# Moving one tile's tail rows forward and issuing 63 matrix products in halves, in a kernel that streams products

## The chip, the cores and the metric

One core of one Trainium2 chip. The metric is the device time of that core in microseconds (us), the lower the better. Times are medians of several executions; a trace of one execution belongs to each kernel. The experiments ran in four batches on four chips (1 to 4, 5 to 8, 9 to 11, and 12), each beside the kernel before on the same chip, so gains are differences within a batch. Before the change the kernel took 476.81 us (median of three runs, 476.67 to 477.1).

## The reference

A cross network of six layers on a batch of 16384 rows by 416 columns, all in bf16:

```python
def reference(x0, ws, bs):            # (16384, 416), (6, 416, 416), (6, 416)
    x = x0
    for l in range(6):
        proj = jnp.einsum('bd,de->be', x, ws[l]) + bs[l]
        x = x0 * proj + x
    return x
```

## The kernel before

The rows are cut into eight groups of 2048, held transposed (columns on the partitions). A group g in a layer l is a job (g, l). 416 columns are three input tiles of 128 and a tail of 32, so an output tile of 128 columns by 2048 rows needs, in four PSUM banks of 512 rows each, twelve full products (three input tiles t, four chunks j) and four products with the 32 tail rows, which use only 32 rows of the array and run side by side (in the trace of before 384 of 447 successive pairs of them start 2 to 5 ns apart, and the rest 215 to 217, the interval of full products):

```python
    def full(g, l, i, banks, first, chunk_major, after_chunk=None, chunks=range(NJ), ts_=range(NT)):
        ...
        for t, j in seq:
            add("pe", lambda h, t=t, j=j: h.matmul(
                bank(banks[j]), wm[l][:, t, ecols], src(t, j, j + 1),
                start=(first and t == 0), stop=(not first and t == NT - 1)),
                reads=[stok(t, j), ("wm", l)], writes=[("ps", banks[j])])
            ...

    def rows32(g, l, i, banks, first, small=False, inner=False):   # the tail rows
        ...                        # small: sixteen 32x32 pieces in place of four products
            add("pe", lambda h, q=q, j=j, r=r: h.matmul(
                bank(banks[j]), w3[l][q, ecols], src[q, :], start=first and not inner,
                stop=not first and not inner,
                tile_position=(r * T32, 0)),
                ...
```

ACT reads a finished tile out of PSUM and adds the bias (L398), DVE multiplies by x0 (L407) and adds x (L412). The kernel's eight banks hold two tiles, so a tile's banks must be read before the tile after the next can begin (two weight loads of before, at 24.54 and 25.55 us, came after 0.51 and 0.89 us of waiting for ACT's reads). Most tiles alternate: full products and then tail rows, next tail rows and then full products, so that two sets of tail rows meet. The first job is followed by the first two tiles of the second group, which have their own function, because their input is still arriving:

```python
    def two_tiles(g, l):
        ...
        bks = [job_banks(), job_banks()]
        for t in (0, 1):
            for i in (0, 1):
                full(g, l, i, bks[i], True, False, ts_=[t])
        full(g, l, 0, bks[0], True, False, ts_=[2])
        rows32(g, l, 0, bks[0], False)
        evacuate(g, l, 0, bks[0], list(range(NJ)), 2)
        finish_tile(g, l)
        rows32(g, l, 1, bks[1], False, inner=True)
        full(g, l, 1, bks[1], False, False, ts_=[2])
        evacuate(g, l, 1, bks[1], list(range(NJ)), 2)
        finish_tile(g, l)
```

At the end two things overlap. The output of the last group but one is turned to rows by transposing DMAs (`ost` from x, `ot` for the tail; ACT copies `ot` into `ost`) and then stored. The last job computes its rows directly and stores them in pieces:

```python
        turn(0); turn(1)                      # ost <- x, transposing DMA     (shortened)
        add("sp", lambda h: h.dma_start_transpose(ot3[:, :, :], x3s[s3][:, :]), ...)
        turn(2, 0, 2); turn(2, 2, NJ)
    ...
        if (g, l) == (LAST, L - 2) and i < NT - 1:
            if i:
                spread("act")                 # ost <- ot, on ACT
            rest_turn(i)                      # x <- x, transposing DMA for the last job
    ...
    store(LAST - 1, 0, 2)                     # out <- ost, the first stores of the end
    store(LAST - 1, 2, NJ)
```

## Time and profile before

| | before |
|---|---|
| time | 476.81 us; with later runs beside the experiments 477.1 |
| span of the profiled execution | 475.1 us |
| PE | 3344 matmuls and 3344 weight loads, busy 99% |
| DVE, ACT | busy 85% and 72% |
| instruction fetches (queue 8) | 26 packets, 0.43 MB |
| DMA | busy 49% of the span on average, but full from 460 to about 473 us |

PE has work in every slice of the profile, so whatever lengthens or shortens PE's stream should move the end. The prediction below shows the lines for that.

### The profile page before, as it was taken

How to read it: one execution, taken by the hardware profiler on the slowest of the kernel's cores; microseconds unless marked ns; L12 is line 12 of the kernel's file. 1: busy time of each engine (PE TensorE's matmuls, PEld its weight loads, DVE VectorE, ACT ScalarE, POOL GpSimd, SP SyncE). 2: the span in 40 equal slices, each digit the busy share in tenths (PEclk: the TensorE clock that was granted, in tenths of full speed). 3: DMA queues.
4: the chain of work that ended last, by engine and by line, in shares of the span. 5: the costliest groups of instructions: out<-in, count | busy, mean ns of one | idle time of the engine just before them, and what ended most of it. 6: DMA issues, size and time to landing. Idle time of an engine off the chain costs nothing.

```text
span 475.1 us, 8338 instructions
## 1 busy us (share of the span) xinstructions
PE 468.5 (99%) x3344; PEld 193.5 (41%) x3344; DVE 404.5 (85%) x699; ACT 342.1 (72%) x372; POOL 6.0 (1%) x15
## 2 busy tenths in 40 slices
PE   9999999999999999999999999999999999999995
PEld 5334444444444444444444444444444444444342
DVE  2888888888888888898889879888888888888896
ACT  4587777777777777777777777777777777777785
POOL 1000000000000000000000000000000000001000
PEclk9999999999999999999999999999999999999999
DMA  8996910720102397379318931980000039025998
GB/s 234 195 165 148 193 49 1 156 67 0 35 1 45 73 219 156 76 157 228 82 31 199 218 87 31 180 256 0 2 12 23 9 63 239 12 46 121 228 181 258
DMA packets 138651, 53.18 MB, mean 112 GB/s; under 512 B 112362, under 2 KB 138100, under 8 KB 138612
## 3 DMA queue, kind: packets, MB, share of 16 engines
q1 hardware_dynamic: 138456, 52.54, 48.9%
q8 instruction: 26, 0.43, 0.4%
q10 hardware_dynamic: 156, 0.11, 0.1%
q14 instruction: 13, 0.11, 0.1%
HBM read 5.97 MB, written 13.63 MB: 41 GB/s over the span
## 4 chain that ended last, share of the span: by engine, by line
PE 98%; ACT 1%; DVE 0%; issue 0%; DVEq 0%; POOL 0%; POOLq 0%
PE ps L460 78%; PE ps L481 7%; PE ps L502 7%; PE ps L858 2%; PE ps L475 1%; PE ps L561 1%; PE ps L581 1%; PE ps L493 1%; ACT tw L398 0%; PE ps L869 0%; PE ps L902 0%; ACT x L913 0%; DVE x L919 0%; DVE x L925 0%; PE ps L907 0%; PE ps L601 0%
## 5 line engine op out<-in xcount | busy, mean ns | idle before, releaser
L398 ACT ACTIVATE tw<-ps,bias 128x1024 bf16<-128x1024 f32 (+1 forms) x295 | 299.8, 1071 | 120.1 <-PE ps L481 81.9
L460 PE MATMUL ps<-x,wm 128*128 128x512 bf16 x1692 | 379.9, 380 | 0.4 <-ACT tw L398 0.4
L460 PEld LDWEIGHTS ps<-x,wm 128*128 128x128 bf16 x1692 | 158.6, 98 | 215.1 <-issue 28.2
L407 DVE TENSOR_TENSOR tw<-tw,x 128x1024 bf16<-128x1024 bf16 (+1 forms) x285 | 192.5, 683 | 53.1 <-ACT tw L398 52.7
L412 DVE TENSOR_TENSOR x<-tw,x 128x1024 bf16<-128x1024 bf16 (+1 forms) x285 | 183.1, 683 | 0.0
L481 PE MATMUL ps<-x,w 32*128 32x512 bf16 x512 | 39.2, 379 | 0.0
L502 PE MATMUL ps<-x,wm 128*32 128x512 bf16 x564 | 33.0, 380 | 0.0
L438 ACT ACTIVATE ts<-ps,bias 128x512 bf16<-128x512 f32 x47 | 28.8, 702 | 0.0
L442 DVE TENSOR_TENSOR x<-ts,x 128x512 bf16<-128x512 bf16 x47 | 18.8, 422 | 2.7 <-DMA x<-x 2.7
L502 PEld LDWEIGHTS ps<-x,wm 128*32 128x32 bf16 x564 | 13.8, 96 | 17.6 <-issue 5.3
L481 PEld LDWEIGHTS ps<-x,w 32*128 32x128 bf16 x512 | 7.8, 92 | 27.6 <-issue 27.1
L440 DVE TENSOR_TENSOR ts<-ts,x 128x512 bf16<-128x512 bf16 x47 | 18.7, 421 | 0.0
L701 POOL COPY ost<-ot 128x512 bf16<-128x512 bf16 x6 | 4.6, 764 | 422.8 <-DMA ot<-x 422.8
L858 PE MATMUL ps<-wm,x 128*128 128x416 bf16 x48 | 9.5, 340 | 0.0
L591 DVE COPY x<-ps 128x512 bf16<-128x512 bf16 x5 | 2.0, 423 | 8.3 <-PE ps L581 8.3
L913 ACT ACTIVATE x<-ps 128x416 bf16<-128x416 f32 x16 | 7.8, 527 | 1.7 <-PE ps L858 1.6
L593 ACT ACTIVATE x<-ps 128x512 bf16<-128x512 bf16 x7 | 3.8, 595 | 5.0 <-PE ps L581 5.0
L858 PEld LDWEIGHTS ps<-wm,x 128*128 128x128 bf16 x48 | 4.3, 98 | 4.2 <-issue 1.0
L493 PE MATMUL ps<-x,w 32*32 32x512 bf16 x188 | 5.9, 374 | 0.0
L475 PE MATMUL ps<-x,w 32*32 32x512 bf16 x208 | 5.6, 385 | 0.0
L919 DVE TENSOR_TENSOR x<-x,x 128x832 bf16<-128x832 bf16 (+1 forms) x10 | 4.9, 502 | 0.6 <-ACT x L913 0.4
L925 DVE TENSOR_TENSOR x<-x,x 128x832 bf16<-128x832 bf16 (+1 forms) x9 | 4.7, 541 | 0.2
(41 smaller groups left out, 33.9 us busy)
## 6 DMA issues: line engine op xcount, KB each, us to landing
out_dram<-ost SPq DMA_DIRECT2D x6, 1664.0 KB, 7.2
x<-x SPq DMA_DIRECT2D x24, 96.0 KB, 2.1
wm<-in_ws_dram SPq DMA_DIRECT2D x6, 312.0 KB, 3.2
x<-in_x_dram SPq DMA_DIRECT2D x8, 208.0 KB, 4.0
x<-in_x_dram SPq DMA_DIRECT2D x4, 416.0 KB, 7.9
out_dram<-ost SPq DMA_DIRECT2D x2, 832.0 KB, 7.1
x<-x SPq DMA_DIRECT2D x22, 64.0 KB, 2.1
out_dram<-x SPq DMA_DIRECT2D x3, 416.0 KB, 5.2
```

What stands on the lines that cost most here:

```text
L398: add("act", lambda h, a=a, w=w, b0=b0: h.activation(tw[r][:, a * CH:(a + w) * CH], psum[:, b0 * CH:(b0 + w) * CH], ACT_F.Identity, bias=b ...
L407: add("dve", lambda h, a=a, e=e: h.tensor_tensor(tw[r][:, a * CH:e * CH], tw[r][:, a * CH:e * CH], x0s[s0][:, i * GC + a * CH:i * GC + e * ...
L412: add("dve", lambda h, a=a, e=e: h.tensor_tensor(xs[so][:, i * GC + a * CH:i * GC + e * CH], tw[r][:, a * CH:e * CH], src(i, a, e), ALU.ad ...
L438: add("act", lambda h: h.activation(ts[r][:, :], bank(b), ACT_F.Identity, bias=bias[:, 3, l:l + 1], scale=1.0), reads=[("ps", b), "bias"], ...
L440: add("dve", lambda h: h.tensor_tensor(ts[r][:, :], ts[r][:, :], x03, ALU.mult), reads=[("ts", r)] + tok0, writes=[("ts", r)], release=True)
L442: add("dve", lambda h: h.tensor_tensor(x3s[so][:, :], ts[r][:, :], res, ALU.add), reads=[("ts", r)] + rtok, writes=[("x3", so), ("x3", so, ...
L460: add("pe", lambda h, t=t, j=j: h.matmul(bank(banks[j]), wm[l][:, t, ecols], src(t, j, j + 1), start=(first and t == 0), stop=(not first a ...
L475: add("pe", lambda h, q=q, j=j, r=r, c=c, o=o: h.matmul(psum[o, banks[j] * CH:(banks[j] + 1) * CH], w3[l][q, i * P + c * T32:i * P + (c + ...
L481: add("pe", lambda h, q=q, j=j, r=r: h.matmul(bank(banks[j]), w3[l][q, ecols], src[q, :], start=first and not inner, stop=not first and no ...
L493: add("pe", lambda h, l=l, b=b, s3=s3, ri=ri, qi=qi, ro=ro, qo=qo: h.matmul(psum[qo, b * CH:(b + 1) * CH], w3[l][qi, NT * P:D], s3[qi, :], ...
L502: add("pe", lambda h, t=t, j=j, src=src, l=l, b=b, ro=ro, qo=qo: h.matmul(psum[qo, b * CH:(b + 1) * CH], wm[l][:, t, NT * P:D], src(t, j, ...
L858: add("pe", lambda h, t=t: h.matmul(bank(b, n=D), xcol(t, j, kk), wm[l][:, t, :], start=(first and t == 0), stop=(not first and t == NT - 1)),
```

## The change

The first part moves the second tile's four products with its middle input tile behind the first tile's tail rows, so that the first tile is complete four products sooner. The second issues 63 full products of three later jobs as two of 256 columns each, with the same weights.

```diff
+    HALVES = ((1, 2), (2, 1), (3, 0))
+    halves = [63]
 ...
         for t, j in seq:
-            add("pe", lambda h, t=t, j=j: h.matmul(
-                bank(banks[j]), wm[l][:, t, ecols], src(t, j, j + 1),
+            n = 1
+            if (g, l) in HALVES and halves[0] and t != (0 if first else NT - 1):
+                halves[0] -= 1
+                n = 2
+            w = CH // n
+            for k in range(n):
+                add("pe", lambda h, t=t, j=j, k=k, w=w: h.matmul(
+                    bank(banks[j])[:, k * w:(k + 1) * w], wm[l][:, t, ecols], src(t, j, j + 1)[:, k * w:(k + 1) * w],
 ...
-        for t in (0, 1):
-            for i in (0, 1):
-                full(g, l, i, bks[i], True, False, ts_=[t])
-        full(g, l, 0, bks[0], True, False, ts_=[2])
+        for i in (0, 1):
+            full(g, l, i, bks[i], True, False, ts_=[0])
+        full(g, l, 0, bks[0], True, False, ts_=[1, 2])
         rows32(g, l, 0, bks[0], False)
         evacuate(g, l, 0, bks[0], list(range(NJ)), 2)
         finish_tile(g, l)
         rows32(g, l, 1, bks[1], False, inner=True)
-        full(g, l, 1, bks[1], False, False, ts_=[2])
+        full(g, l, 1, bks[1], False, False, ts_=[1, 2])
```

More of the change, by code (lines that the diff above doesn't have):

```diff
@@ L459, in full @@
         for t, j in seq:
-            add("pe", lambda h, t=t, j=j: h.matmul(
-                bank(banks[j]), wm[l][:, t, ecols], src(t, j, j + 1),
-                start=(first and t == 0), stop=(not first and t == NT - 1)),
-                reads=[stok(t, j), ("wm", l)], writes=[("ps", banks[j])])
+            n = 1
[6 more added lines that the diff above has]
+                    bank(banks[j])[:, k * w:(k + 1) * w], wm[l][:, t, ecols], src(t, j, j + 1)[:, k * w:(k + 1) * w],
+                    start=(first and t == 0), stop=(not first and t == NT - 1)),
+                    reads=[stok(t, j), ("wm", l)], writes=[("ps", banks[j])])
             if after_chunk and t == NT - 1:
```

## The prediction

> **What bounds the kernel now.** I read the page first: engine shares, then the chain of work that ended last.
>
> ```profile
> span 475.1 us, 8338 instructions
> ...
> PE 468.5 (99%) x3344; PEld 193.5 (41%) x3344; DVE 404.5 (85%) x699; ACT 342.1 (72%) x372; POOL 6.0 (1%) x15
> ...
> PE 98%; ACT 1%; DVE 0%; issue 0%; DVEq 0%; POOL 0%; POOLq 0%
> ```
>
> The matmul engine is the whole path: 98% of the chain that ended last. A busy share says little here, because a matmul's recorded duration (380 ns) overlaps the next one's. So I took the starts of successive matmuls from the trace. Of 1610 successive pairs in which both are main products (line L460, 128 partitions by 512 columns), 1522 stand 215 or 216 ns apart. Of the rest, 83 are 225 to 227 ns, 10 more each; they mostly follow a change of row form (itself a steady 304 to 312 ns) or a wait. After the first 12 us only two are longer: 400 and 779 ns. So from 12 us to 457 us PE streams, except in one place. The timeline of matmuls from 18.5 to 28.3 us (columns: start, length, engine, line, operation, tiles, count, idle before and what ended it):
>
> ```profile
> 18.52 4.49 PE L460 MATMUL ps<-x,wm 128*128 128x512 bf16 x20
> 22.95 0.61 PE L481 MATMUL ps<-x,w 32*128 32x512 bf16 x8
> 23.49 1.66 PE L460 MATMUL ps<-x,wm 128*128 128x512 bf16 x6
> 25.55 2.33 PE L460 MATMUL ps<-x,wm 128*128 128x512 bf16 x10 [0.40 <-ACT tw L398]
> ```
>
> These are the second group's first two tiles, which the change touches: 20 products (both tiles' first two input tiles, and the first tile's third), 8 tail-row products (two sets of four that run side by side), the second tile's last 4 products, and then the first job's next layer. The group of 6 hides the 400 ns interval: its last two already belong to the next layer. The weight loads of the same window show both waits:
>
> ```profile
> 23.49 0.55 PEld L460 LDWEIGHTS ps<-x,wm 128*128 128x128 bf16 x4 [0.42 <-issue]
> 24.54 0.11 PEld L460 LDWEIGHTS ps<-x,wm 128*128 128x128 bf16 x2 [0.51 <-ACT tw L398]
> 25.55 1.84 PEld L460 LDWEIGHTS ps<-x,wm 128*128 128x128 bf16 x10 [0.89 <-ACT tw L398]
> ```
>
> PE wants the four PSUM banks of the first tile again and ACT has not read them yet. The ACT timeline says why:
>
> ```profile
> 23.38 4.28 ACT L398 ACTIVATE tw<-ps,bias 128x1024 bf16<-128x1024 f32 x5 [3.74 <-PE ps L481]
> ```
>
> ACT idled 3.74 us, then got two tiles almost at once, because the tail rows that complete the first tile come at 22.95 us, behind four products of the second. Each 128x1024 read lasts about 1.11 us and the next starts 1.01 us after it: the first pair of banks is free at 23.378 + 1.114 = 24.492, the second at 24.392 + 1.105 = 25.497. PE resumes 55 ns after each, at 24.547 and 25.552.
>
> [...] The trace shows 26 fetches of 16 KB on queue 8, none with a long matmul interval beside it.
>
> **The change part by part.** The order comparison shows that only PE's stream changes; ACT, DVE, POOL and SP keep their order and their waits.
>
> *Part 1, the tail rows earlier.* The second tile's four products of the middle input tile move behind the first tile's tail rows. The total work is the same. The tail rows move forward by 4 x 216 = 864 ns, to 22.083. ACT starts 431 ns after that (23.378 - 22.947 before), at 22.514. The first pair of banks is free at 23.628, the second at 22.514 + 1.014 + 1.105 = 24.633; with the 55 ns, PE may use them from 23.68 and 24.69. When does PE want them? The second tile's tail rows follow, then eight products in one run, the first at 23.490 - 0.864 = 22.626 and the last at 22.626 + 0.226 + 6 x 0.216 = 24.147, where it is now. The next layer then wants the first pair at 24.363 and the second at 24.795. Both banks are free, with 0.68 and 0.11 us to spare. So the two waits vanish, with the 10 ns each left on the product after it: (400 - 216) + 10 + (779 - 216) + 11 = 768 ns. All of it is on PE, hence on the path.
>
> Is anything else in place in time? The third input tile of this group is now wanted at 18.524 + 12 x 0.216, about 21.12; its transfer landed at 19.84, 1.28 us earlier. The tail rows need four copies of DVE that end at 20.08; they are wanted at 22.08. The next layer's weights landed at 21.06. ACT's second tile then starts at about 24.53 in place of 25.39, so ACT and DVE follow PE forward. Later jobs wait for no transfer that PE feels: there is not one long interval from 25.8 to 457 us. Group 2's load does not move with PE, but its last piece lands at 40.4 and its first product comes at about 67.5.
>
> *Part 2, 63 products in halves.* They belong to the three jobs that run from 91 to 125 us. Eight of a tile's twelve products are split, so 63 weight loads and 63 matmuls are added. The added cost is the fixed part of a matmul. From 216 at 512 columns and 175.7 at 416, a column costs 40.3 / 96 = 0.42 ns; [...] An added load (98 ns recorded) fits beside a matmul of 109 ns, as it does beside one of 56. [...] The purpose is not plain to me; nothing in the profile asks for it.
>
> *Sum:* -0.768 + 0.170 = -0.60 us, 0.13% of 476.81: 476.21 us.
>
> **The rivals.**
> 1. *The halves cost more.* If each split costs 12.2 ns, 63 of them eat 768 ns and the time stays 476.8. The 10 ns that a matmul pays after a change of form would be such a cost, if every half paid it. Against it: the 128-column transposes, each with its own load, run at 55 or 56, so a small product as such pays nothing. If a load were not hidden behind 109 ns (98 ns exposed, 63 times), the kernel would be slower by 6.2 - 0.77, about 482.2; the transposes speak clearly against it.
> 2. *The wait moves.* The margin at the second pair of banks is 0.11 us. If the weight load, held until the bank is free, is not complete when its matmul could go, some 0.1 us of the gain is lost: 476.3. If the third input tile lands more than 1.28 us later in some run, PE waits there instead; a whole microsecond of such a wait would undo the gain (477).
> 3. *The gain is swallowed at the end.* The last stores start when DVE has finished, about 1.6 us after PE's last product began (469.58), and land 3 us later. They move with PE, and no wait on a fixed clock stands between; the output traffic of the last 15 us can shift a landing by some tenths. 476.0 to 476.5.
> 4. *The halves give something.* A half has its own weight load, and PE gets no other work; I see nothing to gain, for the streams there have no gap.
>
> **Range and chances.** Three runs of before spread over 0.43 us, as much as the effect. The gain is well pinned (the waits are measured, the banks free in time), the halves' cost is interpolated, and run scatter covers +-0.25. I take 475.8 to 476.8. A change of 2% would be 9.5 us: nothing in the profile can give it, since the waits removed are all that PE has in mid-stream; slower by 2% would need about 160 ns per split product. Chances: faster 0.005, same 0.985, slower 0.01.
>
> **What would show it.** In the new profile: no wait on ACT in the weight loads near 24.5 and 25.5 us; ACT's idle before the first tile 2.9 in place of 3.7 us; the matmuls of the next layer from 24.36 at 216 ns; everything from 28 to 88 us about 0.77 us earlier; halves 109 or 110 ns apart; after 125 us the stream 0.6 us earlier than before. It would be wrong if a wait for a transfer appears at about 21 us, if halves stand over 115 ns apart, or if the stream is ahead at 125 us and the end is not.

The sum came to -0.60 us: -0.768 for the two waits and +0.170 for the halves, 63 times 2.7 ns. The starts in the trace of before give nearly the same (an estimate made afterwards): successive products stand 215.83 ns apart with 512 columns (mean of the 1522 pairs at 215 or 216), 175.86 with 416 (37 pairs at 175 or 176) and 55.80 with 128 (45 pairs at 55 or 56). So a column costs (215.83 - 55.80) / 384 = 0.4168 ns, and 215.83 - 512 x 0.4168 leaves 2.4 ns that do not depend on the columns. A half of 256 columns then takes 109.1 ns; a second product in place of one adds the 2.4 ns, and 63 of them add 0.15 us.

## More of the kernel before

The columns are the stretch, its length, the busy time of PE, its weight loads, DVE, ACT and POOL with the number of instructions, the granted clock, the mean busy share of the DMA engines, and what they moved in GB/s. Kernel before:

```profile
460.00:464.00 4.00, 4.00 (x38) 2.10 (x37) 3.57 (x9) 3.36 (x8) 0.00 (x0) 1.00 1.08 254
464.00:468.00 4.00, 4.00 (x35) 1.64 (x33) 3.75 (x8) 3.30 (x7) 0.00 (x0) 1.00 1.09 325
468.00:472.00 4.00, 1.92 (x11) 0.88 (x9) 3.48 (x9) 2.07 (x4) 0.00 (x0) 1.00 0.99 308
```

From 460 us on the DMA engines are as full as PE (shares of 1.08, 1.09 and 0.99), and they stay full after PE has stopped.

## The result, and the profile after

The changed kernel took 475.76 us (median of six runs, 475.33 to 477.81), the kernel before 477.08 beside it (476.67 to 477.6). The ratio is 0.9977, with a 95% interval of 0.9960 to 0.9993: the same within 2%, as predicted. The gain is 1.32 us where the prediction had 0.60.

The first trace of the changed kernel happened to be its slowest run (477.81). Its matmul timeline from 5.9 to 11 us (columns: start, length, engine, line, operation, tiles, count, idle before and what ended it) says why:

```profile
6.46 2.72 PE L471 MATMUL ps<-x,wm 128*128 128x512 bf16 x6 [0.48 <-DMA wm<-in_ws_dram]
8.97 2.18 PE L592 MATMUL ps<-ident,x 128*128 128x128 bf16 x24
```

and the kernel before in the same place:

```profile
5.92 1.51 PE L460 MATMUL ps<-x,wm 128*128 128x512 bf16 x6
7.28 1.50 PE L581 MATMUL ps<-ident,x 128*128 128x128 bf16 x24
```

The first layer's weights landed half a microsecond later (6.33 against 5.79 us), PE idled 0.48 us, and the clock was granted in full only from 10.38 us, so six products took 2.72 in place of 1.51 us. That start cost 2.35 us. In the other twelve traces (and in that of before) the full clock came between 3.76 and 6.68 us. None of this belongs to the change, so the changed kernel was run and traced again (first experiment: 475.70 us), and that trace stands for "after" below. Its page:

```profile
span 474.0 us, 8464 instructions
...
PE 468.7 (99%) x3407; PEld 199.9 (42%) x3407; DVE 404.8 (85%) x699; ACT 341.7 (72%) x372; POOL 6.0 (1%) x15
...
q8 instruction: 26, 0.43, 0.4%
...
PE 97%; ACT 1%; DVE 1%; DMA 1%; issue 0%; DVEq 0%; POOL 0%; POOLq 0%
```

There are 63 more matmuls and 63 more loads, and PE is busy 0.2 us longer. The chain that ended last now has 1% of DMA in it, which the kernel before had not. The second group's first tiles in its matmul timeline:

```profile
18.78 3.63 PE L471 MATMUL ps<-x,wm 128*128 128x512 bf16 x16
22.34 0.61 PE L492 MATMUL ps<-x,w 32*128 32x512 bf16 x8
22.88 4.49 PE L471 MATMUL ps<-x,wm 128*128 128x512 bf16 x20
```

its weight loads:

```profile
22.88 1.84 PEld L471 LDWEIGHTS ps<-x,wm 128*128 128x128 bf16 x10 [0.42 <-issue]
24.94 1.94 PEld L471 LDWEIGHTS ps<-x,wm 128*128 128x128 bf16 x10 [0.22 <-ACT tw L398]
```

and ACT:

```profile
22.77 4.28 ACT L398 ACTIVATE tw<-ps,bias 128x1024 bf16<-128x1024 f32 x5 [2.88 <-PE ps L492]
```

Sixteen products, the eight of the tail rows, and then twenty products without a break. The tail rows come at 22.34, the predicted 22.08 plus 0.25 us by which this execution started later. ACT's idle fell from 3.74 to 2.88 us (predicted 2.9). The first weight-load wait is gone; of the second 0.22 us is left, on a load that runs ahead of its matmul, and no long interval of matmuls comes of it. This part went as predicted. The halves, by form:

```profile
L471 PE MATMUL ps<-x,wm 128*128 128x512 bf16 x1629 | 366.2, 380 | 0.0
...
L471 PE MATMUL ps<-x,wm 128*128 128x256 bf16 x126 | 15.1, 273 | 0.0
```

126 halves; the recorded 273 ns overlap the next. From the starts, halves stand 109 or 110 ns apart, each with its own weight load, and one split product costs 2.5 ns more than a whole.

So where is the rest? I took from each trace four instants: the start of the same 128x32 product near 447 us ("stream", as a shift against before), the first of the end's stores ("first store", where its shift exceeds that of the stream), and the time from that store to the last landing of a store ("drain"). The change of span is the sum of stream, first store and change of drain.

| us | stream | first store | drain | span |
|---|---|---|---|---|
| before | 0 | 0 | 13.70 | 475.07 |
| after | -0.35 | +0.62 | 12.34 | 473.99 |

The stream term is 0.25 (start) - 0.77 (two waits) + 0.16 (halves) = -0.36. That is the prediction's sum, intact. But then the first store comes 0.62 us later than PE's stream would have it, and everything after it takes 1.36 us less. The end does not simply move with PE. The DMA view of 460 to 475 us (queues: packets, MB, share; then each store: count, size, us from issue to landing) of the kernel before:

```profile
q1 hardware_dynamic: 5631, 3.68, 87.4%
...
q8 instruction: 1, 0.02, 0.4%
...
out_dram<-ost SPq DMA_DIRECT2D x2, 832.0 KB, 7.1
out_dram<-x SPq DMA_DIRECT2D x3, 416.0 KB, 5.2
...
out_dram<-x ACTq DMA_DIRECT2D x1, 104.0 KB, 3.0
```

and of the changed kernel:

```profile
q1 hardware_dynamic: 5850, 3.74, 86.2%
...
out_dram<-ost SPq DMA_DIRECT2D x2, 832.0 KB, 5.4
out_dram<-x SPq DMA_DIRECT2D x3, 416.0 KB, 4.0
...
out_dram<-x ACTq DMA_DIRECT2D x1, 104.0 KB, 1.9
```

Every store lands 1.1 to 1.7 us sooner, down to the last one (3.0 to 1.9). And there is no line for queue 8. In the kernel before, one packet of instructions was fetched in this window, at 463.78 us; in the changed kernel that last fetch is at 452.29. The packet is 16 KB. In the trace the landing of each of these stores is sixteen signals, as many as the core has DMA engines on the page. I call them its shares and count the store as landed with the last. That each is one engine's part, and that the packet, being one, occupies one of the sixteen engines, is inferred: the trace names no engine of a packet. In before, fifteen shares of the first store had landed by 465.41 and the sixteenth at 466.93; of the last store, fifteen by 473.47 and one at 474.59. In the changed kernel the last store's shares are at 473.38 and 473.50. So one share in sixteen was 1.1 to 1.5 us behind from the fetch to the end.

Why does the fetch move? Matmuls and weight loads are PE's instructions; the page counts 6688 on 26 packets, 257 to a packet. (I call what a packet brings a block, and take it for about 256 instructions, an estimate from that count. Kernel 4 below bears it out: 256 more instructions of PE bring one more packet and leave the last one nearly where it was, 461.62 against 461.21 us in kernel 2. That queue 8 is PE's is borne out by kernels 5 to 8, where only PE's stream changes and these packets move.) The 63 halves add 126 instructions in front of the last block. Each block boundary is then reached earlier in the work, by an estimated 126 x 0.07 us = 9 us (475 us over 6688 instructions); observed are 11.5. That was the theory to test: **the halves do nothing for the arithmetic; they are worth about 0.6 us because they push PE's last instruction fetch out of the final stores.** It would explain the half of the gain that the stream does not show. The price shows too. At 452.29 the packet falls among the transposing transfers that feed the first store. DMA view of 448 to 455 us in 40 slices of 0.175 us (busy tenths; GB/s), kernel before:

```profile
DMA  9999900299999999999993000029999999999999
GB/s 260 208 215 186 53 7 9 54 279 291 271 291 288 295 285 290 288 269 262 243 210 56 0 0 0 0 64 215 218 212 211 208 221 219 217 217 215 218 184 218
```

and the changed kernel:

```profile
DMA  9990029999999999999200006999931000899999
GB/s 212 173 57 7 9 54 281 295 267 294 287 293 291 285 290 274 269 236 212 47 0 0 0 0 165 219 202 186 60 3 9 9 10 9 177 287 293 290 287 295
...
q8 instruction: 1, 0.02, 0.8%
```

The second has a hole that the first has not: six slices (453 to 454 us) in which 3 to 60 GB/s move. One engine may still have had to work off its rest; that is not shown. The queue's own timeline shows the same hole as a late issue. Before (columns as above):

```profile
447.99 5.39 SPq L672 DMA_TRANSPOSE ost<-x  x2
453.43 1.69 SPq L680 DMA_TRANSPOSE ot<-x  x1
...
460.89 1.13 SPq L708 DMA_DIRECT2D out_dram<-ost  x2
```

After:

```profile
447.63 6.56 SPq L683 DMA_TRANSPOSE ost<-x  x2
454.24 1.26 SPq L691 DMA_TRANSPOSE ot<-x  x1
...
461.16 1.13 SPq L719 DMA_DIRECT2D out_dram<-ost  x2
```

The pair of transposes takes 6.56 in place of 5.39 us, and the first store goes out at 461.16 in place of 460.89 although PE is 0.35 us ahead.

### The profile page after: what moved, and what is told of

Same layout as the page of the kernel before. It is cut to its first block, busy times and chain, and to the rows that moved or that the text cites. A ratio compares the mean times of both kernels' runs of the same rounds, so it can differ in the third digit from the quotient of the medians.

```text
span 476.0 us, 8464 instructions
## 1 busy us (share of the span) xinstructions
PE 470.3 (99%) x3407; PEld 200.9 (42%) x3407; DVE 404.2 (85%) x699; ACT 342.0 (72%) x372; POOL 6.3 (1%) x15
## 4 chain that ended last, share of the span: by engine, by line
PE 96%; DMA 2%; ACT 1%; DVE 1%; SPq 0%; issue 0%; DVEq 0%
PE ps L471 78%; PE ps L492 7%; PE ps L513 7%; PE ps L868 1%; PE ps L486 1%; DMA wm<-in_ws_dram 1%; ACT tw L398 1%; PE ps L504 1%; PE ps L592 1%; DMA ot<-x 1%; DVE tw L407 0%; PE ps L879 0%; ACT x L923 0%; DVE x L929 0%; DVE x L935 0%; PE ps L912 0%
## 5 line engine op out<-in xcount | busy, mean ns | idle before, releaser
L471 PE MATMUL ps<-x,wm 128*128 128x512 bf16 (+1 forms) x1755 | 380.9, 373 | 0.5 <-DMA wm<-in_ws_dram 0.5
L471 PEld LDWEIGHTS ps<-x,wm 128*128 128x128 bf16 x1755 | 165.3, 98 | 210.0 <-issue 29.3
```

Source lines behind the costliest of these rows:

```text
L471: add("pe", lambda h, t=t, j=j, k=k, w=w: h.matmul(bank(banks[j])[:, k * w:(k + 1) * w], wm[l][:, t, ecols], src(t, j, j + 1)[:, k * w:(k ...
```

## The experiments

The rivals of this theory: (R1) the halves help in themselves, by some effect on PE, PSUM or the clock; (R2) the reorder is worth 1.3 us and the halves nothing; (R3) what differs from the prediction is scatter. Kernel n below is that of experiment n. All twelve kernels gave correct results, timed in five rounds against the kernel before (477.06 to 477.21 beside them).

**1. The changed kernel again.** No edit.

> The changed kernel once more, for a profile of an ordinary run (the first profile began with a matmul clock that stayed low until 10.4 us). Theory A (the halves pay by moving the last instruction fetch of the matmul engine, 16 KB, out of the last output stores, where in the kernel before it held one DMA engine's share back by 1.12 us: 473.47 to 474.59): 0.61 us less in the stream and some 0.9 less at the end, -1.5 us in all; the last store's 16 shares land within 0.4 us. Theory B (only the stream counts, the rest was scatter of the start): -0.61 us.

Measured: 475.70 us against 477.08, -1.38, ratio 0.9969 (0.9948 to 0.9989). The gain repeats. Its interval (-0.5 to -2.5 us) alone would still reach the predicted -0.60, but two medians of -1.32 and -1.38 make R3 poor. The trace is the one used above.

**2. The reorder alone.** The `two_tiles` part of the diff; `full` as before.

> Tail rows moved, no halves. Both theories: the two waits go, -0.77 us against the kernel before. They differ against the changed kernel: A says this one is slower than it by about 0.8 us, with the last fetch of the matmul engine back at about 463 us and one share of the last store about 1.1 us behind the other fifteen; B says it is faster than it by 0.16 us.

Measured: 476.25 against 477.08, -0.83, ratio 0.9981 (0.9962 to 1.0). In the trace the two waits are gone (-0.767 us of stream), the last fetch is at 461.21, inside the stores, and the drain is 14.03 us: the last store takes 3.3 us to land (3.0 in before).

The median is what was predicted of the reorder. The interval reaches from 0 to -1.8 us and would not by itself exclude 1.3 us. But the trace gives the reorder 0.77 us of stream and no shorter drain, and kernels 3 and 6 gain without it: with them R2 falls.

**3. The halves alone.** The `full` part of the diff; `two_tiles` as before.

> 63 products in halves, the old order of the first two tiles. A: +0.16 for the halves, -0.9 to -1.1 for the last store: -0.8 us against the kernel before, last fetch at about 454 us. B: +0.16 us, the two waits near 25 us still there.

Measured: 476.37 against 477.08, -0.71, ratio 0.9980 (0.9962 to 0.9999). The stream is 0.16 us longer, as predicted, and both waits are still there. Weight loads:

```profile
24.43 0.11 PEld L471 LDWEIGHTS ps<-x,wm 128*128 128x128 bf16 x2 [0.51 <-ACT tw L398]
25.44 1.84 PEld L471 LDWEIGHTS ps<-x,wm 128*128 128x128 bf16 x10 [0.89 <-ACT tw L398]
```

Yet the kernel is faster: the last fetch is at 451.85, no queue-8 packet falls among the stores, and the drain is 12.30 us. So the halves gain about 0.7 us while they lengthen the stream.

**4. Twice as many halves.**

```diff
-    HALVES = ((1, 2), (2, 1), (3, 0))
-    halves = [63]
+    HALVES = ((1, 2), (2, 1), (3, 0), (0, 4), (1, 3), (2, 2))
+    halves = [128]
```

> The new order with 128 products in halves: 256 instructions more, one whole 16 KB block, so that the last fetch falls again where it was before, about 463 us. A: -0.77 + 0.32 = -0.45 us against the kernel before, 1.1 slower than the changed kernel, one share of the last store about 1 us late. B: -0.45 against before too, but only 0.16 slower than the changed kernel.

Measured: 476.26 against 477.08, -0.82, ratio 0.999 (0.9967 to 1.0014). The 128 halves cost 0.32 us of stream. 256 more instructions bring a 27th fetch, and it falls at 461.62. DMA view, 460 to 475 us:

```profile
q8 instruction: 1, 0.02, 0.5%
...
out_dram<-x ACTq DMA_DIRECT2D x1, 104.0 KB, 2.7
```

The drain is back at 13.39 us. The interval of the ratio is wide, through two long runs (478.84 and 477.31). Run by run the two kernels are apart: all six of this one took 476.19 us or more, five of six of kernel 1 took 475.82 or less. With more halves of the same kind the gain of the drain is gone, which R1 cannot say.

**5 and 6. No halves, but about as many more instructions.** PE gets 134 waits that are satisfied long before (on a semaphore that POOL raised at the start), spread over the same three jobs (the loop below asks for more; 134 further semaphore instructions of PE stand in the trace, and the numbers of waits below are counted in this way); in 5 with the new order of `two_tiles`, in 6 with the old.

```diff
             for op in self.queue[e]:
+                if op.fn == "pad":
+                    handle.wait_ge(sems["pool"], 1)
+                    continue
 ...
+    PADS = ((1, 2), (2, 1), (3, 0))
+    pads = [126]
 ...
         for t, j in seq:
+            n = min(2, pads[0]) if (g, l) in PADS else 0
+            pads[0] -= n
+            for _ in range(n and 2 * n + 1):
+                add("pe", "pad")
```

> The new order, no halves; instead 134 waits that are long satisfied stand in the matmul engine's stream before products of the same three jobs. They lengthen the instruction stream about as the halves do and give the array no work. A (the last fetch's place counts): last fetch at about 452 us, the last store's shares within 0.4 us (-1.1), the new wait of ACT for the transfer into ot still there (+0.37), the two waits near 25 us gone (-0.77): -1.5 us against the kernel before, about 0.16 faster than the changed kernel. C (the halves themselves help, as smaller products): -0.77 only, with a late share in the last store.

> The old order with the 134 satisfied waits, no halves. A: +0.37 - 1.1 = -0.7 us against the kernel before, with the two waits near 25 us still there. C: 0.0 us.

Measured: 475.51 against 477.06 for the new order, -1.55, ratio 0.9967 (0.9955 to 0.998); 476.47 for the old, -0.59, ratio 0.9988 (0.9976 to 1.0001). The waits cost nothing of stream (0.00). DMA view of kernel 6, 460 to 475 us, which has no queue-8 line:

```profile
out_dram<-ost SPq DMA_DIRECT2D x2, 832.0 KB, 5.4
...
out_dram<-x ACTq DMA_DIRECT2D x1, 104.0 KB, 1.9
```

Kernel 6 computes exactly what before computes, in the same order, and its stores land as in the changed kernel (drain 12.31 us, last fetch at 452.00). Its own interval touches 1.0; with kernel 5, which has no halves and the whole gain, R1 falls: it is the number of instructions, not the halves. Kernel 5's interval (-0.95 to -2.1 us) also leaves out the -0.77 of its stream, which is the end of R3.

**7 and 8. Other numbers of waits, new order.** 184 and 64 (both with job (0, 4) as a further place).

> The new order with 174 or more satisfied waits (4 us more of shift): last fetch at about 448.5 us, before the transfers into ost and ot that ACT waits for in the changed kernel. A: last store's shares together (-1.1), no wait of ACT for ot, or a shorter one (0 to +0.37), -0.77: -1.5 to -1.9 us against the kernel before, and the fastest of all. B (stream only): -0.77.

> The new order with some 60 satisfied waits: last fetch at about 458 us, beside the transposing transfers of the last two jobs and still ahead of the output stores that begin at 460. A: no late share in the last store (-1.1), no wait of ACT for ot, but the transfers that the last additions need may land up to 1 us late (0 to +0.5): -1.3 to -1.9 us. B: -0.77.

Measured: 476.36 (-0.70, ratio 0.9985, 0.9973 to 0.9998) with 184; 475.84 (-1.22, ratio 0.9971, 0.9958 to 0.9985) with 64. The expectation for 184 was wrong: I had hoped to move the fetch ahead of the transposes as well, and instead the stream crossed into a further block. The page of that kernel:

```profile
span 474.5 us, 8522 instructions
...
q8 instruction: 27, 0.44, 0.4%
```

Its 27th fetch is at 467.07, among the stores, and the drain is 13.35. The miss fits the mechanism by another route. With 64 the fetch is at 459.44, just ahead of the stores: the drain is short (12.40) but the last transposes are held up, and the first store is 0.83 us later than the stream; the gain is a little under the -1.3 to -1.9 expected. These kernels and kernel 5 differ in the number and place of the waits alone and ran in one batch: all five runs with 64 (475.36 to 475.86) and all five with 134 (475.33 to 475.57) are faster than all five with 184 (475.99 to 476.59).

**9. Kernel 5 with the copy `ost` from `ot` on POOL.** By then I held that the first-store delay works through PE: ACT waits for `ot` ahead of the copy (0.7 us in the changed kernel), DVE and PE behind it.

```diff
-                spread("act")
+                spread("pool")
```

> The 134 satisfied waits and the new order, and the copy from ot to ost for the seventh group on POOL in place of ACT, so that ACT does not stand behind the transfer into ot. Theory A: PE gains the 0.4 us that the wait costs it, -0.77 - 1.1 = -1.9 us against the kernel before, about 475.1 us, the fastest. If the time stays at that of the run with the waits alone (-1.5), the wait of ACT was not on the path.

Measured: 475.35 against 477.08, -1.73, ratio 0.9963 (0.9951 to 0.9976). This is the fastest median, but 0.16 below kernel 5, which ran on another chip, and with overlapping intervals. It is not shown to be better. PE lost as much as in kernel 5 (0.41 us); DVE's additions were slower; POOL's copy is the one edit, and how it would slow them is not shown. DVE timeline, kernel 9:

```profile
456.16 1.70 DVE L415 TENSOR_TENSOR x<-tw,x 128x1024 bf16<-128x1024 bf16 x2
```

Two additions in 1.70 us, where kernel 5 has 1.29 (one of them 1.10 in place of 0.68). And the first store, and with it the end, stayed where it was in kernel 5 against the stream (+0.67).

**10. 158 waits, new order**, between 134 and 184, to see how far the block limit is.

> The new order with 158 satisfied waits: between the 134 that help and the 184 that needed one block more. Last fetch at about 450.5 us, 26 fetches in all, last store together. A: ACT's wait for ot some 0.5 us in place of 0.77, so PE loses 0.2 in place of 0.4: -1.6 to -1.7 us against the kernel before. If there are 27 fetches, the last falls near 467 us again and the time is that of 184 waits (-0.7).

Measured: 476.25 (-0.83, ratio 0.9983, 0.9969 to 0.9996). 27 fetches already, the last at 468.16; the drain is 13.41. The first expectation failed and the one for 27 fetches held. So the limit lies between 134 and 158 more instructions.

**11. 96 fewer PE instructions, new order.** Four tiles take their tail rows as whole products in place of 32x32 pieces.

```diff
+    skip = [0]
 ...
-            rows32(g, l, i, banks, False, mode[n] == "F1")
+            f1 = mode[n] == "F1"
+            skip[0] += f1
+            rows32(g, l, i, banks, False, f1 and not 3 <= skip[0] <= 6)
```

> The new order and 96 instructions fewer for the matmul engine in place of more: four of the thirteen tiles whose tail rows go in 32x32 pieces take them in 32x128 pieces. A: the block that the kernel before fetches last is not fetched at all (25 fetches, the last at about 445 us), the last store's shares land together and ACT does not wait for ot: -0.77 - 1.1, with some +0.1 to +0.4 for the four tiles: -1.5 to -1.8 us against the kernel before. If the last store's share is still late with no fetch near it, A is wrong.

Measured: 477.14 (+0.06, ratio 1.0006, 0.9992 to 1.0019). The four tiles cost 0.44 us of stream, which eats much of the reorder's gain. The last fetch is not gone but 7.7 us later than in kernel 2 (468.90), still among the stores, and the drain is 13.46. The expectation was wrong by 1.5 us: it had counted on one fetch fewer.

**12. Kernel 5 with the copy on ACT after the last tile's reads.** It takes the wait for `ot` off PE's path altogether.

```diff
-            if i:
-                spread("act")
             rest_turn(i)
+    spread("act")                     # after the loop
```

> As the run with 134 satisfied waits, but ACT makes the copy from ot to ost after the four reads of the last tile in place of ahead of them (POOL, tried before, slowed a DVE add from 0.68 to 1.10 us and so gave nothing). The transfer into ot has landed by then, so no read of PSUM waits for it. A: the 0.4 us that PE loses in the last ten us goes, -0.77 - 1.1 = -1.9 us against the kernel before, about 475.1 us; the copy itself may push the next copies by 0.2 us, then -1.7. If it stays at -1.5, the loss of PE there has another cause than ACT's wait.

Measured: 475.73 against 477.21, -1.48, ratio 0.9966 (0.9953 to 0.998). The waits from 455 to 461 us (engine, line, what it waited for: us in total, times, longest) in the changed kernel:

```profile
ACT ost L710 <- DMA ot<-x: 0.7, 1, 0.7
...
```

and in kernel 12:

```profile
ACT x L921 <- PE ps L866: 0.6, 1, 0.6
PEld ps L866 <- DVE x L415: 0.4, 1, 0.4
```

ACT no longer waits for `ot`, and PE loses nothing there: its last products stand against the stream as in before, within 0.01 us. The time did not follow: -1.48 against -1.55 of kernel 5. I had expected about -1.9. So the loss on PE was not on the path; the first store (+0.66) and the 12.29 us after it are the end. That part of my theory fell.

**All of them together.** Estimate of each gain from its trace, without the scatter of the start: stream (the waits -0.77, the halves, in kernel 11 the tail rows) + first store + change of drain. The start is left out since each trace has its own (-0.17 to +0.37 us, and +2.35 in the first trace of after).

| kernel | last fetch, us | stream | first store | drain | sum against before | measured |
|---|---|---|---|---|---|---|
| before | 463.78 | 0 | 0 | 13.70 | 0 | 0 |
| 2 reorder | 461.21 | -0.77 | -0.01 | 14.03 | -0.45 | -0.83 |
| 4 128 halves, reorder | 461.62 | -0.45 | 0.00 | 13.39 | -0.76 | -0.82 |
| 7 184 waits | 467.07 | -0.77 | +0.16 | 13.35 | -0.96 | -0.70 |
| 10 158 waits | 468.16 | -0.77 | +0.28 | 13.41 | -0.78 | -0.83 |
| 11 96 fewer | 468.90 | -0.33 | +0.28 | 13.46 | -0.29 | +0.06 |
| 1 after | 452.29 | -0.61 | +0.62 | 12.34 | -1.35 | -1.38 |
| 3 halves | 451.85 | +0.16 | +0.64 | 12.30 | -0.60 | -0.71 |
| 5 134 waits | 451.44 | -0.77 | +0.66 | 12.34 | -1.47 | -1.55 |
| 6 134 waits, old order | 452.00 | 0 | +0.67 | 12.31 | -0.72 | -0.59 |
| 8 64 waits | 459.44 | -0.77 | +0.83 | 12.40 | -1.24 | -1.22 |
| 9 copy on POOL | 451.15 | -0.77 | +0.67 | 12.44 | -1.36 | -1.73 |
| 12 late copy | 451.71 | -0.77 | +0.66 | 12.29 | -1.52 | -1.48 |

The kernels fall into two classes with nothing between: a last fetch after the first store, drain 13.35 to 14.03; a last fetch before it, drain 12.29 to 12.44. The sums, each from one execution, agree with the measured medians within 0.15 us for eight of the twelve kernels, and within 0.38 for the rest.

The traces hold two more signs. The late share begins at the fetch: in kernels 7, 10 and 11, whose last fetch falls in mid-drain (467.07, 468.16, 468.90), every store that had landed by 0.9 us after the fetch's start had its last share at most 0.15 us behind the other fifteen, and in every later store it is 0.86 to 1.19 us behind. In the eight traces with an earlier last fetch, the one of the changed kernel's slow start included, no share of any store is more than 0.43 us behind. And in these same three kernels the fetch before the last falls among the first transposes (449.39, 449.61 and 450.19); it may be why their first store is 0.16 to 0.28 us late.

## Why the prediction was right or wrong

**The class and the sum of PE's stream were right.** The two waits on ACT vanished and gave 0.767 us in every kernel with the new order (predicted 0.768). The halves cost 2.5 ns each, 0.158 us for 63 (the forecast had 2.7 and 0.170), and 0.32 for 128. No wait came in place of the ones removed: the input tile was there, and the margin of 0.11 us at the second pair of banks held.

**The place of the halves was wrong, without effect.** It put their jobs at 91 to 125 us; in the trace the halves run from 76 to 102. The same kind of slip stands in "its first product comes at about 67.5": by the order of jobs in the code that product begins at about 58.5 us, still well after the 40.4 of its last piece. And the last stores start 2.0 us after PE's last product began (471.62 against 469.58), not 1.6. Nothing in the sum rests on these.

**The size of the gain was wrong by a factor of two, and the step that failed is rival 3's sentence "They move with PE, and no wait on a fixed clock stands between".** The end moves with PE only as far as the first store (in kernels 2 and 4 that store follows the stream within 0.01 us). From the first store on it is a transfer of about 12.3 us with full DMA engines, or of 13.4 to 14.0 us if an instruction packet falls into it. The busy shares of 460 to 472 us (1.08, 1.09, 0.99) were in the profile of before and were not used; I had looked for the bound in the chain of waits alone, which names PE for 98%. Two terms are missing from the sum: +0.62 us for the later first store, and -1.36 us for the shorter drain. With them, -0.61 + 0.62 - 1.36 = -1.35, against -1.32 and -1.38 measured. That 475.76 us still comes out at the low end of the stated 475.8 to 476.8 is luck as far as the end is concerned: the two missing terms partly cancel, and neither was foreseen.

**Rival 4's "I see nothing to gain" and "The purpose is not plain to me" were wrong for the same reason.** I looked for the effect of the halves on the engine that runs them, found only a cost, and stopped. Their effect is 350 us later on another unit. I did check the 26 fetches, but asked only whether PE waits for them. It does not: in before only two intervals of matmuls after 12 us are long, at 24.15 and 24.77 us, and the nearest fetches are at 13.38 and 29.93. The question not asked was what a fetch holds up among the transfers. Net, the halves are worth about 0.16 + 0.62 - 1.36 = -0.58 us as worked out from the traces, and -0.71 us as measured alone.

**Afterwards my own theory failed in two places.** I put the first-store delay down to PE's wait behind ACT (kernel 12 refutes it: PE lost nothing there and the delay stayed; kernel 9 could not decide, since PE lost 0.41 us in it as in kernel 5), and I expected that more waits would go on gaining (kernels 7 and 10 show the next block).

**What stays open.** The fetch's position in the work is shown by its time in twelve traces, not by an experiment that moves a fetch alone, with the number of instructions kept. How the delay passes from the transposes to the first store is read from the queue's timeline and not tested. A kernel whose last fetch meets neither the transposes nor the stores should gain about 0.77 + 1.36 = 2.1 us (an estimate from the traces); none was reached, because the step to an earlier fetch brings a 27th, and the 96 instructions that could be saved at little cost are too few. The kernel with the copy on POOL is the fastest measured (475.35), not a proven improvement over the changed one (475.70).

## What to carry to other kernels

Where a kernel ends in a stretch of full DMA engines, ask what else uses those engines there: here one 16 KB packet of instructions made one share of every later store about 1 us late (0.86 to 1.19 us in kernels 7, 10 and 11). Where a change added or removed instructions of the longest stream, its fetches moved to other moments (the last from 463.78 to 452.29 us with the 126 of the halves), and two kernels with the same arithmetic differed by 0.2% (kernels 5 and 7: 475.51 and 476.36 us); compare where the last fetch falls before crediting the edit. And when the chain of waits gives one engine nearly all of the path, still read the busy shares of the last stretch: here, once the first store was out, the end came 12.3 us later however soon PE was done (kernels 5 and 12).
